# Rounding half of g by GpSimd DMAs, weights' signs by ScalarE, a state updated in place, and another written order

## The chip, the cores and the metric

The kernel runs on one core of one Trainium2 chip. A core has TensorE (PE in the profile; its weight loads are PEld), VectorE (DVE), ScalarE (ACT), GpSimd (POOL) and SyncE (SP), each with a queue that it works through in order, and 16 DMA engines that move data for all of them. The metric is device microseconds of one execution. Before the change the median of three runs was 516.24 us (515.70 to 516.78).

## The reference, cut to what matters

There are two stages. The first is a gated linear recurrence for 4 batches and 8 heads over 768 tokens of 48 numbers; the second a gated two-layer network on 3072 tokens.

```python
for t in range(S):
    state = alpha[:, :, t, :, None] * state + einsum('bhd,bhe->bhde', k[:, :, t], v[:, :, t])
    y[:, :, t] = einsum('bhd,bhde->bhe', q[:, :, t], state)
x = y.transpose(0, 2, 1, 3).reshape(3072, 384)
h = x @ w_in                                   # 384 x 2048
sp = maximum(h, 0) + log1p(exp(-abs(h)))       # softplus
g = h * erf(sp)
out = g @ w_out                                # 2048 x 384
```

q, k, v and alpha are float32; the two weights come as float64.

## The kernel before

**Tiles.** The tokens are cut into 24 chunks of 128 (64 tokens of two batches) and 12 blocks of 256 (two chunks). The 2048 hidden columns of a block are 4 groups of 512 rows by 256 tokens (a tile of 128 x 1024), each of two halves (128 x 512).

**High and low parts.** Every large product runs on TensorE with operands rounded to float32r. A number is split into a rounded part and the rest, and three products are added: high x high, low x high, high x low. `hm` (line 532) is one half's h: 3 x 6 matmuls of 256 columns into a PSUM ring of two. `om` (617) is one half's share of the output: 3 x 4 matmuls of 384 columns.

**One chunk** (`la` to `xe`, lines 296 to 465): loads; two scans over alpha (`sb`, `sa`); scaled k and q (`kk`, `qq`); k transposed (`pn`, then `kn` by ScalarE or `kd` by VectorE); the state scaled by the chunk's whole decay (`td`) and put to use for the outputs (`qt`); products within the chunk (`ps`, masked by `mk`, `sv`); the state's new part (`pu`) added (`ta`). `outputs` (372) opens a PSUM tile with `qt` or `sv` and closes it with the other; between the two stands a `relay`, a memset on GpSimd that waits for the first. The result goes to x by `xh` (the rounded part, by ScalarE) and `xl` (the rest, by VectorE); a second way to the rest, `xp` with `xe` (TensorE subtracts, ScalarE copies), is defined, and the order does not use it. The state has two tiles per batch pair: `td` writes the second from the first, `ta` the first from the second.

**One group** (lines 532 to 631): `hm`, copied by `he` (ScalarE) or `hd` (VectorE); `u`, `n1`, `n2`, `n3`, `g` on ScalarE, 1024 columns each; `ma`, `mb`, `z1`, `z2` on VectorE, `z2` leaving g in the h tile. `u` and `g` need one table set of ScalarE, `n1` to `n3` another; `need` (259) loads a set where the one before was the other. g's high part, `gh`, is written by `ga` (ScalarE) or `gd` (VectorE), the rest by `gl` (VectorE), both into rings of two tiles, and `om` follows. `oe` (ScalarE) or `ob` (VectorE) copies out and `od` stores.

**Weights** (644 to 727). 12 tiles of w_in (`i`, 512 columns) and 16 of w_out (`o`, 384 columns) are loaded as pairs of 32-bit words (`wl`) and made float32 by bits: `wy` scales the upper word, `wc` (ScalarE) or `wv` (VectorE) takes three bits from the lower one, `wa` shifts and joins them, `wb` puts the sign back. `wh` (ScalarE) or `wk` (VectorE) rounds; the low part comes by `wq` (VectorE) or by `wp` (TensorE) with `we` (ScalarE). `wd` and `wf` are defined and not used in the order: `wd` writes the upper 16-bit half of each word, which leaves the sign, `wf` the lower half, with the three bits.

**Order.** `ORDER` (line 31) lists all 1664 steps. Each of the queues of TensorE, VectorE, ScalarE and SyncE issues its instructions in just that order (`Queue`, 203). GpSimd's instructions are not held to it. `dw` steps are matmuls on a constant whose result nobody uses. The rest of the program (`general`) runs only where a check of the values fails; with these inputs it does not.

Of the kernel before, what the change touches and what calls it, by code (L numbers as in the profile page):

```python
# [31 lines left out]
la_0 wli_2 wyi_2 wci_2 wli_3 wyi_3 wci_3 sb_0 rc_0 sa_0 wai_2 wbi_2 whi_2 wli_0 wyi_0 wci_0 wai_3 wbi_3 dw_14  # L32
wpi_2 lk_0 kk_0 wli_4 whi_3 wyi_4 lq_0 ic_0 la_1 wci_4 wei_2 wai_0 wbi_0 pn_0 kn_0 whi_0 wpi_3 wei_3 qq_0 dw_3
ps_0 wai_4 wli_7 wci_7 wli_6 sb_1 mk_0 wyi_7 wbi_4 wai_7 wci_6 wyi_6 wli_8 wpi_0 rc_1 whi_4 dw_7 wpi_4 wbi_7
whi_7 wai_6 sa_1 wbi_6 wyi_8 wci_8 wai_8 lv_0 ic_1 wei_4 wli_5 lq_1 qq_1 wei_0 lk_1 pu_0 kk_1 wli_1 lv_1 wci_5
sv_0 xh_0 wyi_5 xl_0 wbi_8 wpi_7 wai_5 whi_6 ps_1 mk_1 wci_1 wyi_1 wai_1 whi_8 wei_7 wlo_2 wpi_6 wvo_2 sv_1
wyo_2 xh_1 wbi_1 whi_1 wei_6 wpi_8 ta_0 la_2 sb_2 wao_2 wlo_12 wyo_12 dw_1 wpi_1 pn_1 wei_8 wbi_5 whi_5 wpi_5
wli_11 wco_12 kn_1 wbo_2 wei_1 wli_9 who_2 rc_2 ic_2 xl_1 wei_5 sa_2 hm_0_0_0 wao_12 td_2 lq_2 wyi_11 wbo_12
wlo_0 lk_2 wco_0 wqo_2 lv_2 wli_10 who_12 hm_0_0_1 kk_2 pu_1 qq_2 ps_2 wqo_12 wyo_0 wao_0 wci_9 wci_11 wai_11
he_0_0_0 la_3 sb_3 wbi_11 wbo_0 wci_10 wyi_10 he_0_0_1 wai_10 wyi_9 wai_9 lk_3 hm_0_1_0 mk_2 qt_2 u_0_0 rc_3  # L40
hm_0_2_0 sv_2 lq_3 ta_1 wbi_9 sa_3 wlo_1 wbi_10 he_0_1_0 whi_11 whi_9 who_0 td_3 wqi_11 la_4 qq_3 wvo_1 kk_3
wqo_0 he_0_2_0 whi_10 wyo_1 wao_1 sb_4 wqi_9 n1_0_0 xh_2 xl_2 pn_2 kn_2 n2_0_0 wqi_10 ic_3 hm_0_1_1 he_0_1_1
n3_0_0 hm_0_2_1 he_0_2_1 wbo_1 rc_4 who_1 pu_2 ps_3 wlo_3 wyo_3 lq_4 lk_4 wlo_7 mk_3 ta_2 qt_3 ma_0_0 g_0_0 sa_4
wlo_6 mb_0_0 wqo_1 hm_0_3_0 z1_0_0 wco_3 wao_3 lv_3 sv_3 xh_3 xl_3 kk_4 pn_3 he_0_3_0 wyo_7 hm_0_3_1 kn_3 ic_4
z2_0_0 td_4 lk_5 he_0_3_1 la_5 wco_7 wco_6 hm_1_0_0 qq_4 wlo_9 wyo_6 sb_5 u_0_1 wao_7 wbo_3 ga_0_0_0 gl_0_0_0
hm_1_1_0 he_1_0_0 ga_0_0_1 gl_0_0_1 wao_6 u_0_2 n1_0_1 pu_3 ps_4 n1_0_2 rc_5 n2_0_1 qt_4 om_0_0_0 hm_1_0_1 wbo_7
# [97 lines left out]
def gla_moe(ctx: ExitStack, tc: tile.TileContext, q, k, v, alpha, w_in, w_out, out):  # L144
    nc = tc.nc
# [57 lines left out]
    class Queue:  # L203
# [3 lines left out]
        def __getattr__(self, name):  # L207
# [57 lines left out]
    for t in Ts[0] + Ts[1]:  # L265
        nc.gpsimd.memset(t, 0.0)  # L266
# [377 lines left out]
    class Weight:  # L644
# [66 lines left out]
        def wk(self):  # L711
            self.wh(on_dve)
# [234 lines left out]
```

## Time and profile before

| | |
|---|---|
| runs, median (lowest to highest) | 516.24 us (515.70 to 516.78) |
| profiled execution, first to last instruction (span) | 513.9 us |
| runs' median over that span | 2.3 us |
| TensorE busy, matmuls | 504.0 us (98%) |
| VectorE busy | 488.2 us (95%), 655 instructions |
| ScalarE busy | 465.8 us (91%), 637 instructions, 64 of them table loads |
| GpSimd busy | 6.5 us (1%) |
| granted clock of TensorE | 1.000 |

The profiled execution has no other time of its own than its span, so the last rows compare it with the runs. A duration is that of one instruction from its start until its result is written; neighbours on an engine overlap by some 0.07 us, so the distance of two starts is what an instruction takes from its queue. A matmul's end is modelled; its start is a record. "idle before" is an engine's idle time and what ended it. All calls pass through a helper, so most instructions bear its line, 211, and are told apart by their tiles: `acc` is the output's PSUM, `h` that of h, `hs` the h and g tiles, `py` and `both` those of the recurrence.

### The profile page before, as it was taken

Reading aid. Unit: us, or ns where it says so; the run is one execution under the profiler, and the core shown is the slowest. Engines: PE = TensorE matmul, PEld = TensorE weight load, DVE = VectorE, ACT = ScalarE, POOL = GpSimd, SP = SyncE. Lnnn points to the kernel's source line nnn. Section 1 sums busy time; section 2 is a strip of 40 time slices with the busy share of each in tenths; the row PEclk is TensorE's granted clock in tenths of the full one; section 3 lists DMA queues with packets and bytes.
Section 4 is the critical chain, followed back from the end, with each engine's and each line's share of the span. In section 5 each row is a group of like instructions: output and inputs, shape, how many; then the busy total and the mean of one; then the engine's idle time right before and its main releaser. Section 6 shows DMA issues by size and latency. Waiting matters only on the chain.

```text
span 513.9 us, 16869 instructions
## 1 busy us (share of the span) xinstructions
PE 504.0 (98%) x7465; PEld 481.7 (94%) x7465; DVE 488.2 (95%) x655; ACT 465.8 (91%) x637; POOL 6.5 (1%) x41
## 2 busy tenths in 40 slices
PE   6999999999999999999999999999999999999996
PEld 6689999999999999999999999999999999999996
DVE  6999999999999999999999999999998999999894
ACT  6999999999999989999898888899988899898992
POOL 3000000000000000000000000000000000000000
PEclk9999999999999999999999999999999999999999
DMA  8954363321121032122023211301231310000000
GB/s 324 401 200 176 117 188 131 97 81 60 58 74 44 22 99 78 45 73 83 23 78 107 80 41 60 85 15 44 68 111 54 90 58 32 3 1 32 0 32 34
DMA packets 21387, 43.69 MB, mean 85 GB/s; under 512 B 2368, under 2 KB 5440, under 8 KB 21312
## 3 DMA queue, kind: packets, MB, share of 16 engines
q1 hardware_dynamic: 21312, 42.59, 25.4%
q8 instruction: 59, 0.97, 0.8%
q14 instruction: 16, 0.13, 0.1%
HBM read 37.86 MB, written 4.72 MB: 83 GB/s over the span
## 4 chain that ended last, share of the span: by engine, by line
PE 64%; DVE 18%; ACT 12%; issue 4%; DMA 1%; POOL 1%; DVEq 0%; POOLq 0%; ACTq 0%
PE acc L211 29%; PE h__112 L211 13%; PE h__111 L211 12%; PE both L211 4%; PE py L211 4%; DVE t L211 2%; DVE gl__104 L211 1%; ACT L211 1%; DVE gl__103 L211 1%; DVE w__98 L211 1%; DVE w__100 L211 1%; PE warm L211 1%; ACT w__97 L211 1%; DMA s__87<-in_moe_w_out_dram 1%; DVE w__97 L211 1%
## 5 line engine op out<-in xcount | busy, mean ns | idle before, releaser
L211 ACT ACT_TABLE_LOAD x64 | 82.1, 1283 | 1.9 <-PEq L901 0.9
L211 PE MATMUL acc<-wo_hi,gh__102 128*128 128x384 f32 x192 | 44.7, 346 | 0.1
L211 PE MATMUL acc<-wo_hi,gh__101 128*128 128x384 f32 x192 | 43.9, 348 | 0.1
L211 PE MATMUL acc<-wo_lo,gh__102 128*128 128x384 f32 x192 | 43.0, 337 | 0.2 <-DVE wo_lo L211 0.2
L211 PE MATMUL acc<-wo_hi,gl__104 128*128 128x384 f32 x192 | 43.1, 337 | 0.0
L211 PE MATMUL acc<-wo_lo,gh__101 128*128 128x384 f32 x192 | 41.6, 336 | 0.0
L211 PE MATMUL acc<-wo_hi,gl__103 128*128 128x384 f32 x192 | 41.6, 337 | 0.0
L211 PEld LDWEIGHTS acc<-wo_lo,gh__102 128*128 128x128 f32 x192 | 34.2, 188 | 0.5 <-DVE wo_lo L211 0.5
L211 PEld LDWEIGHTS acc<-wo_hi,gl__104 128*128 128x128 f32 x192 | 34.3, 188 | 0.0
L211 PEld LDWEIGHTS acc<-wo_hi,gl__103 128*128 128x128 f32 x192 | 34.0, 188 | 0.2 <-DVE gl__103 L211 0.2
L211 PEld LDWEIGHTS acc<-wo_lo,gh__101 128*128 128x128 f32 x192 | 34.1, 188 | 0.0
L211 PEld LDWEIGHTS acc<-wo_hi,gh__101 128*128 128x128 f32 x192 | 31.6, 188 | 1.9 <-DVE gh__101 L211 0.4
L211 PEld LDWEIGHTS acc<-wo_hi,gh__102 128*128 128x128 f32 x192 | 32.6, 188 | 0.8 <-DVE gh__102 L211 0.2
L211 DVE TENSOR_TENSOR_SCAN B<-raw_a,back 128x520 f32<-128x520 f32 x24 | 29.6, 1233 | 4.0 <-POOL T L266 3.9
L211 DVE TENSOR_TENSOR_SCAN A<-raw_a,start 128x520 f32<-128x520 f32 x24 | 29.6, 1233 | 0.2
L211 ACT ACTIVATE s__88<-s__88 128x1024 f32<-128x1024 f32 x22 | 23.2, 1056 | 1.0 <-DVE t L211 0.9
L211 ACT ACTIVATE s__86<-s__86 128x1024 f32<-128x1024 f32 x20 | 21.2, 1058 | 1.9 <-DVE t L211 1.8
L211 PE MATMUL h__112<-x_hi__107,wi_hi 128*128 128x256 f32 x144 | 21.7, 286 | 0.3 <-ACT wi_lo L211 0.3
L211 PE MATMUL h__111<-x_hi__107,wi_hi 128*128 128x256 f32 x144 | 21.4, 284 | 0.0
L211 PE MATMUL h__111<-x_hi__108,wi_hi 128*128 128x256 f32 x144 | 21.1, 282 | 0.0
L211 PE MATMUL h__112<-x_hi__108,wi_hi 128*128 128x256 f32 x144 | 21.1, 282 | 0.0
L211 PE MATMUL h__112<-x_lo__109,wi_hi 128*128 128x256 f32 x144 | 21.0, 281 | 0.0
(338 smaller groups left out, 1420.5 us busy)
## 6 DMA issues: line engine op xcount, KB each, us to landing
raw_a<-in_alpha_dram SPq DMA_DIRECT2D x24, 260.5 KB, 2.8
raw_k<-in_k_dram SPq DMA_DIRECT2D x24, 256.0 KB, 3.1
raw_q<-in_q_dram SPq DMA_DIRECT2D x24, 256.0 KB, 3.3
raw_v__113<-in_v_dram SPq DMA_DIRECT2D x12, 256.0 KB, 3.3
raw_v__114<-in_v_dram SPq DMA_DIRECT2D x12, 256.0 KB, 3.6
out_dram<-o__106 SPq DMA_DIRECT2D x12, 192.0 KB, 2.0
out_dram<-o__105 SPq DMA_DIRECT2D x12, 192.0 KB, 2.6
s__85<-in_moe_w_out_dram SPq DMA_DIRECT2D x4, 384.0 KB, 3.7
```

What stands on the lines that cost most here:

```text
L211: ins = made(*args, **kw)
```

## The change

48 of the 96 high parts of g are written by `gh`, a DMA that GpSimd issues (from float32 to float32r, 256 KB from SBUF to SBUF); 27 stay with ScalarE (51 before) and 21 with VectorE (45). Their ring has four tiles in place of two. GpSimd gets an ordered queue as well, in which the `gh` and the `relay` memsets stand. Of the 28 weights 20 get sign and low bits by `wd` and `wf` and need no `wb`; the rounding goes mostly to VectorE (`wk` 17, from 1), and the low part of 7 comes by `wp` and `we` (9 before), of 21 by `wq` (19). Four chunks take `xp` and `xe` in place of `xl`. The state has one tile per batch pair: `td` and `ta` update it in place. A group's h tile is taken from its ring by the first `he` (the first `hm` before), so either half can come first. The order is another one, of 1666 steps.

```diff
-    gp = Ring(gpool, gh=([P, 2, TB], F32R, 2), gl=([P, 2, TB], F32R, 2), o0=([P, DM], F32, 1), o1=([P, DM], F32, 1))
+    gp = Ring(gpool, gh=([P, 2, TB], F32R, 4), gl=([P, 2, TB], F32R, 2), o0=([P, DM], F32, 1), o1=([P, DM], F32, 1))
...
-    queues = [Queue(e) for e in (nc.tensor, nc.vector, nc.scalar, nc.sync)]
-    pe, dve, act, sp = queues
+    queues = [Queue(e) for e in (nc.tensor, nc.vector, nc.scalar, nc.sync, nc.gpsimd)]
+    pe, dve, act, sp, pool = queues
...
-            dve.tensor_tensor(out=Tv[self.m][1], in0=Tv[self.m][0], in1=ae.unsqueeze(3).broadcast_to([P, NI, NP, D]), op=ALU.mult)
+            dve.tensor_tensor(out=Tv[self.m], in0=Tv[self.m], in1=ae.unsqueeze(3).broadcast_to([P, NI, NP, D]), op=ALU.mult)
...
-                self.relay = nc.gpsimd.memset(relay, 0.0)
+                self.relay = pool.memset(relay, 0.0)
...
-                dve.tensor_tensor(out=Tv[self.m][0], in0=Tv[self.m][1], in1=U, op=ALU.add)
+                dve.tensor_tensor(out=Tv[self.m], in0=Tv[self.m], in1=U, op=ALU.add)
...
+        def to_hi(self, g, half, copy):
             gg = self.hs[g][:, half * 512 : (half + 1) * 512]
             gh = self.pl.gp.tile([P, 2, TB], F32R, name="gh", tag="gh")
-            act.activation(gh.rearrange("p a t -> p (a t)"), gg, AF.Copy)
+            copy(gh.rearrange("p a t -> p (a t)"), gg)
             self.gg[g, half] = gg, gh
 
+        def gh(self, g, half):
+            self.to_hi(g, half, lambda out, in_: pool.dma_start(out=out, in_=in_))
+
+        def ga(self, g, half):
+            self.to_hi(g, half, on_act)
...
+
+        def wm(self):
+            pool.dma_start(out=self.hi, in_=self.z)
```

`wm` stands in the program and not in the order. Two lines of the new order, the first and the first with `gh`:

```
dw_14 la_0 wli_2 wci_2 sb_0 wyi_2 wli_0 rc_0 sa_0 lk_0 wli_3 ic_0 wfi_0 wai_2 wyi_0 kk_0 wlo_3 wbi_2 wdi_0 la_1 wai_0
rc_5 hm_1_2_0 ta_3 sa_5 he_1_2_0 wao_7 gh_0_0_0 sv_4 lq_7 kk_5 xh_4 wqo_1 gl_0_0_0 la_6 pn_4 hm_1_2_1 td_5 om_0_0_0
```

## Rows read from the trace of the kernel before

**Rows 1.** The page, part 1: busy us, share, instructions of each engine.
```profile
PE 504.0 (98%) x7465; PEld 481.7 (94%) x7465; DVE 488.2 (95%) x655; ACT 465.8 (91%) x637; POOL 6.5 (1%) x41
```
**Rows 2.** Stretches: length; busy us (instructions) by engine; clock, DMA share, GB/s.
```profile
0.00:20.00 20.00, 15.64 (x195) 12.66 (x196) 15.51 (x23) 15.60 (x30) 4.38 (x19) 1.00 0.92 353
20.00:40.00 20.00, 19.35 (x349) 14.91 (x348) 20.00 (x36) 19.97 (x42) 0.10 (x1) 1.00 0.68 242
```
**Rows 3.** Waits of TensorE's weight loads, 28.8 to 120 us: total, times, longest.
```profile
PEld h__112 L211 <- ACT wi_lo L211: 0.9, 1, 0.9
...
PEld h__111 L211 <- ACT hs__94 L211: 0.2, 1, 0.2
```
**Rows 4.** Timeline of TensorE at the first `hm`: start us, length us, instruction.
```profile
28.88 0.99 PE L211 MATMUL h__112<-x_hi__107,wi_hi 128*128 128x256 f32 x6 [0.26 <-ACT wi_lo L211]
```
**Rows 5.** Timeline of TensorE at its end.
```profile
509.33 0.51 PE L211 MATMUL acc<-wo_hi,gl__104 128*128 128x384 f32 x2
```
**Rows 6.** Timeline of TensorE, 108 to 116 us: starts of an `hm` and two `om`.
```profile
108.88 0.87 PE L211 MATMUL h__111<-x_hi__107,wi_hi 128*128 128x256 f32 x6
...
111.00 0.87 PE L211 MATMUL acc<-wo_hi,gh__101 128*128 128x384 f32 x4
...
113.12 0.87 PE L211 MATMUL acc<-wo_hi,gh__102 128*128 128x384 f32 x4
```
**Rows 7.** Groups by line: count, busy us, mean ns of one, idle before.
```profile
L211 PE MATMUL py<-raw_q,T 48*32 48x64 f32 x1408 | 18.9, 224 | 0.0
```
**Rows 8.** Timeline of VectorE, 104 to 117 us.
```profile
104.82 1.22 DVE L211 SCALAR_TENSOR_TENSOR w__99<-t,w__99 128x1024 f32<-128x1024 f32 x1
105.96 0.55 DVE L211 TENSOR_TENSOR wo_lo<-w__97,wo_hi 128x384 fp32r<-128x384 f32 x1
...
111.25 0.42 DVE L211 CAST gh__102<-hs__92 128x512 fp32r<-128x512 f32 x1
...
112.05 1.23 DVE L211 TENSOR_TENSOR_SCAN A<-raw_a,start 128x520 f32<-128x520 f32 x1
113.20 0.67 DVE L211 TENSOR_TENSOR gl__104<-hs__92,gh__102 128x512 fp32r<-128x512 f32 x1
...
114.38 0.68 DVE L211 TENSOR_TENSOR raw_k<-raw_k,B 128x512 f32<-128x512 f32 x1
114.98 0.55 DVE L211 TENSOR_TENSOR T<-T,B 128x384 f32<-128x384 f32 x1
115.45 1.22 DVE L211 TENSOR_TENSOR t<-s__86,w__99 128x1024 f32<-128x1024 f32 x1
```
**Rows 9.** Timeline of ScalarE, 13 to 24 us.
```profile
13.33 1.23 ACT L211 ACTIVATE w__97<-hs__94 128x512 int32<-128x512 uint8 x2
14.45 1.25 ACT L211 ACTIVATE w__98<-hs__95 128x512 int32<-128x512 uint8 x2
```
**Rows 10.** Waits over the whole span: VectorE's first instruction.
```profile
DVE B L211 <- POOL T L266: 3.9, 1, 3.9
```
**Rows 11.** Groups by line: ScalarE's table loads, and one group of `ga`.
```profile
L211 ACT ACT_TABLE_LOAD x64 | 82.1, 1283 | 1.9 <-PEq L901 0.9
...
L211 ACT ACTIVATE gh__102<-hs__93 128x512 fp32r<-128x512 f32 x6 | 3.8, 629 | 2.7 <-DVE hs__93 L211 2.7
```
**Rows 12.** DMA issues: count, KB each, median us from issue to landing.
```profile
raw_v__114<-in_v_dram SPq DMA_DIRECT2D x12, 256.0 KB, 3.6
out_dram<-o__106 SPq DMA_DIRECT2D x12, 192.0 KB, 2.0
out_dram<-o__105 SPq DMA_DIRECT2D x12, 192.0 KB, 2.6
...
hs__95<-in_moe_w_in_dram SPq DMA_DIRECT2D x2, 512.0 KB, 7.0
```
**Rows 13.** Waits over the whole span: the `relay` memsets.
```profile
POOL relay L395 <- PE py L211: 439.8, 22, 32.3
```

More of the change, by code (lines that the diff above doesn't have):

```diff
@@ L37 @@
[L37 to L46, printed above, removed]
@@ new lines @@
+z2_4_2 gl_4_1_0 om_4_1_0 ta_13 ga_4_2_0 mk_14 gl_4_2_0 xl_13 z1_4_3 gl_4_0_1 ic_15 u_5_2 n2_5_0 hd_5_3_0 ga_4_2_1
+om_4_2_0 sa_15 n3_5_0 qq_15 om_4_0_1 n2_5_1 ma_5_0 pn_14 mb_5_0 qt_14 kn_14 n1_5_2 ps_15 n3_5_1 z2_4_3 pu_14 hd_5_3_1
+td_15 sv_14 ma_5_1 lq_16 gl_4_2_1 ga_4_3_1 gl_4_3_1 u_5_3 hm_6_1_1 g_5_0 hm_6_1_0 mb_5_1 he_6_1_1 z1_5_0 mk_15
+he_6_1_0 la_16 gh_4_3_0 u_6_1 od_3_0 om_4_2_1 sb_16 g_5_1 n2_5_2 z2_5_0 n1_5_3 hm_6_0_0 rc_16 z1_5_1 gd_5_0_0 z2_5_1
+hm_6_2_1 om_4_3_1 ic_16 gl_4_3_0 sa_16 om_4_3_0 gh_5_1_1 od_3_1 n3_5_2 n1_6_1 he_6_0_0 n2_5_3 xh_14 oe_4_1 lk_16
@@ new lines @@
+ma_10_0 z1_10_2 he_11_0_1 g_10_0 z2_10_2 f1 om_9_2_1 u_11_0 gh_10_2_0 od_8_1 z2_10_1 mb_10_0 n1_11_0 om_9_0_1
+hm_11_2_0 ga_9_2_0 gl_9_2_0 ma_10_3 hd_11_2_0 hd_11_1_0 n2_11_0 z1_10_0 mb_10_3 om_9_2_0 ga_10_1_1 n3_11_0 ob_9_1
+oe_9_0 ma_11_0 g_10_3 hm_11_1_1 hm_11_2_1 gh_10_2_1 hd_11_1_1 gl_10_2_0 z1_10_3 g_11_0 gl_10_1_1 he_11_2_1 om_10_2_0
+z2_10_3 om_10_1_1 u_11_2 gl_10_2_1 om_10_2_1 z2_10_0 u_11_1 od_9_0 mb_11_0 n1_11_1 hm_11_3_1 hm_11_3_0 ga_10_0_0
+gh_10_3_1 od_9_1 gl_10_0_0 ga_10_0_1 n2_11_1 z1_11_0 gd_10_1_0 n3_11_1 z2_11_0 om_10_0_0 n1_11_2 he_11_3_1 gl_10_3_1
@@ new lines @@
+ma_11_1 mb_11_1 gl_10_0_1 n2_11_2 n3_11_2 om_10_0_1 he_11_3_0 g_11_1 gh_10_3_0 om_10_3_1 ma_11_2 z1_11_1 z2_11_1
+g_11_2 gl_10_1_0 gh_11_0_1 mb_11_2 gl_10_3_0 u_11_3 om_10_1_0 om_10_3_0 z1_11_2 n1_11_3 ob_10_1 n2_11_3 gl_11_0_1
+gh_11_0_0 gl_11_0_0 oe_10_0 z2_11_2 f2 ga_11_1_1 f3 ga_11_1_0 n3_11_3 om_11_0_1 om_11_0_0 od_10_0 gl_11_1_1 gh_11_2_0
+ga_11_2_1 gl_11_1_0 ma_11_3 om_11_1_0 mb_11_3 om_11_1_1 od_10_1 g_11_3 z1_11_3 gl_11_2_0 z2_11_3 om_11_2_0 gh_11_3_1
+gl_11_2_1 gd_11_3_0 om_11_2_1 gl_11_3_0 om_11_3_0 gl_11_3_1 om_11_3_1 oe_11_1 ob_11_0 od_11_1 od_11_0
@@ L262, in need @@
             act.preload_act_table_set(name)
-    Ts = [[at.tile([P, NI * NP * HD], F32, name="T", tag=f"T{m}{n}", bufs=1) for n in range(2)] for m in range(M)]
-    for t in Ts[0] + Ts[1]:
+    Ts = [at.tile([P, NI * NP * HD], F32, name="T", tag=f"T{m}", bufs=1) for m in range(M)]
+    for t in Ts:
         nc.gpsimd.memset(t, 0.0)
-    Tv = [[t.rearrange("p (i a d) -> p i a d", i=NI, a=NP)[:, :, :, :D] for t in pair] for pair in Ts]
+    Tv = [t.rearrange("p (i a d) -> p i a d", i=NI, a=NP)[:, :, :, :D] for t in Ts]
     both = ps_at.tile([P, 2, 512], F32, name="both", tag="b")
     pe.matmul(
-        out=both[:, 1, NP * TC : NP * (TC + D)], lhsT=ident, rhs=Ts[0][0][:, : NP * D],
+        out=both[:, 1, NP * TC : NP * (TC + D)], lhsT=ident, rhs=Ts[0][:, : NP * D],
         start=True, stop=True,
@@ L402, in left @@
                 r0, at0 = (par ^ i) * HD, (i * NP + pair) * HD + d0
-                return Ts[self.m][1][r0 : r0 + D, at0 : at0 + 32], r0
+                return Ts[self.m][r0 : r0 + D, at0 : at0 + 32], r0
             self.outputs(left, lambda i, par, pair: self.Q[(par ^ i) * HD : (par ^ i) * HD + D, pair, i, :])
@@ L533, in hm @@
             x_hi, x_lo = self.x
-            if half == 0:
-                self.hs[g] = self.pl.h.tile([P, GT * TB], F32, name="hs", tag="hs")
             self.ph = self.pl.ph.tile([P, 512], F32, name="ph", tag="h")
@@ L549, in he @@
         def he(self, g, half, copy=on_act):
+            if self.hs[g] is None:
+                self.hs[g] = self.pl.h.tile([P, GT * TB], F32, name="hs", tag="hs")
             sl = slice(half * 512, (half + 1) * 512)
@@ L594, in z2 @@
             )
-        def ga(self, g, half):
+        def to_hi(self, g, half, copy):
             gg = self.hs[g][:, half * 512 : (half + 1) * 512]
             gh = self.pl.gp.tile([P, 2, TB], F32R, name="gh", tag="gh")
-            act.activation(gh.rearrange("p a t -> p (a t)"), gg, AF.Copy)
+            copy(gh.rearrange("p a t -> p (a t)"), gg)
             self.gg[g, half] = gg, gh
+        def gh(self, g, half):
+            self.to_hi(g, half, lambda out, in_: pool.dma_start(out=out, in_=in_))
+        def ga(self, g, half):
+            self.to_hi(g, half, on_act)
         def gd(self, g, half):
-            gg = self.hs[g][:, half * 512 : (half + 1) * 512]
-            gh = self.pl.gp.tile([P, 2, TB], F32R, name="gh", tag="gh")
-            dve.tensor_copy(out=gh.rearrange("p a t -> p (a t)"), in_=gg)
-            self.gg[g, half] = gg, gh
+            self.to_hi(g, half, on_dve)
         def gl(self, g, half):
```

185 lines of the change are left out of this document (86 added, 99 removed).

## The prediction, made before the changed kernel ran

> **What bounds the kernel now.** I read the page's busy shares first, then the stretches, the waits of TensorE, and its timeline at two places. TensorE is busy 98% of the span, VectorE 95%, ScalarE 91% [rows 1]; three engines at the wall say that the share of none of them settles it, so the stretches come next. In the first 20 us TensorE has 15.64 us of work recorded, part of it `dw` matmuls that compute nothing, and from 20 us on it is full, at granted clock 1.00, the higher of its levels [rows 2]. The waits of its weight loads from 28.8 to 120 us come to 2.4 us in five rows, 0.9 us the largest (the first and the last stand in [rows 3]). So behind the first `hm` (which starts at 28.88 us [rows 4]) TensorE hardly stops. The last matmul ends at 509.84 us [rows 5]: 509.84 - 28.88 = 480.96 us for what follows the first `hm`. The kernel is therefore two terms: how late the first `hm` comes, and the 481 us behind it, in which VectorE must keep up closely enough.
>
> I check that by summing TensorE's steps behind that point in the written order. One `hm` (18 matmuls) goes from 108.88 to 111.00, one `om` (12 matmuls) from 111.00 to 113.12 [rows 6]; 96 of each make 407 us. The 22 `qt` are busy 18.9 us, 0.86 each [rows 7]; by the distance of their starts the attention steps take a little less, `qt` 0.84, `sv` 0.89, `ps` 0.57, `pu` 0.57 and `pn` 0.54 us (five such groups, of which one stands). With 20 to 22 of each the whole is 478.7 us, 2.3 us under the 480.96 taken.
>
> **How I sum the other two engines.** An instruction's slot is the distance between two starts, less than its duration, as neighbours overlap. On VectorE: 1.14 us for 1024 columns (104.82 to 105.96), 1.15 for a scan (112.05 to 113.20), 0.60 for 512 (114.38 to 114.98), 0.47 for 384 (114.98 to 115.45), 0.36 for a cast of 512, which the trace records at 0.42 [rows 8]. On ScalarE two conversions of 512 take 1.12 us, 0.56 each (13.33 to 14.45) [rows 9]; I use 0.48 to 0.56 for 512 columns by kind and three quarters of that for 384.
>
> **Term 1: ScalarE's queue ahead of the first `hm`.** Before, the last that it waits for there is `we` of weight i1; after, `xe` of chunk 1. Counting ScalarE's steps ahead of it, before to after: `wc` 10 to 2, `wd` and `wf` 0 to 5 each, `we` 8 to 7, `wh` 9 to 1, `wy` 11 to 10, `xe` 0 to 2, `ic` 2 to 3. That is nine fewer of 512 columns (9 x 0.52 = 4.7) and three more of 384 (3 x 0.42 = 1.3), so 22.3 us become 19.0 us, -3.3. The 16-bit half writes (`wd`, `wf`) have no row. The nearest is `wc`, which also reads one byte in eight, at 0.56 us; I take that, and as the far bound twice it. VectorE's queue to the same place goes from 22.1 to 20.1 us (ten `wb` become two, six casts take the place of `wh`), so ScalarE stays last. TensorE's work behind the point goes from 478.7 to 478.0 (two `xp` more, one `ps` and one `pu` fewer; the three `wp` saved, net two, lie ahead of it, where TensorE waits anyway). By this term alone the end moves by -3.3 - 0.7 = -4.0 us.
>
> **Term 2: VectorE's queue up to the first `om` of block 1.** This is where VectorE is tightest. Before, the second `gl` of that group runs from 113.20 us [rows 8] and its `om` from 113.12 [rows 6], whose last four matmuls want it: hardly any margin. VectorE's slots up to it sum to 108.5 us, and with its start at 3.92 us [rows 10] to 112.4, against 113.87 in the trace. After, up to the first `gl` of the same group: `wb` 28 to 8 (-10.4), `xl` 7 to 3 (-1.9), `gl` 10 to 9 (-0.6); against it 16 more casts `wk` (+5.1), `wq`/`wv` (+1.8), and attention that now runs earlier, `sb` and `rc` +1, `kk` +2, `qq`, `mk`, `ta`, `kd`, `gd` +1, `td` +2 (+5.9). Sum 108.4: the same. But TensorE has less left behind it: `hm` 74 to 72, `om` 87 to 88, one `pn`, `ps`, `qt`, `sv` fewer: -4.24 + 2.10 - 2.84 = -5.0. So this term moves by -5.1, to 502.9 from 508.0; the first term stands at 501.9 from 505.9. The later one decides: -5.1.
>
> **What is off that path.** ScalarE loses 24 `ga` (0.63 us recorded, 0.52 in slots: -12.5) and gets ten more table loads (63 to 73 switches in the written order, 1.29 us each by 1283 ns recorded: +12.9) [rows 11], so the DMAs pay for the tables. VectorE loses 24 `gd`, 10 us in all by the whole balance. Both gains lie mostly after 165 us, where TensorE is behind by its own sums: they buy no time, only margin. The state in place makes `ta` wait for TensorE's `qt`; in 18 of 20 chunks `pu`, for which `ta` waits anyway, stands behind `qt` on TensorE, and in the other two 8 and 16 us of matmuls stand between `qt` and `ta`: nothing, and if that cover went, one `qt` (0.84 us). In the last steps the second `o` goes to VectorE, but both output DMAs queue behind ScalarE's copy: some 0.3 us either way, put at zero.
>
> **The DMAs that round g.** 48 `gh` are issued by GpSimd; the trace has none. Let L be the time from the end of `z2` to data for `gl`: GpSimd's wake, issue, 256 KB through the DMA engines, and the wait's end. Nearest rows: 192 KB out of SBUF land 2.0 and 2.6 us after SP issues them, 256 KB loads 3.6, and at the slow end 512 KB loads 7.0 [rows 12]. As 256 KB move between two places in SBUF I take the SBUF rows plus 64 KB and GpSimd's own issue, L = 3.2 us; bounds 2.0 and 7.0. While L passes, VectorE needs other work: the slots between `z2` and `gl` in the new order, for the 16 `gh` up to 165 us, are 3.9, 10.0, 3.4, 4.0, 8.6, 6.4, 2.9, 3.8, 2.8, 2.7, 3.3, 4.0, 4.6, 5.2, 3.3, 12.6 us. What L lacks there is VectorE standing still with all that is queued behind: 0.4 + 0.4 + 0.5 at L = 3.2, of which the last two fall where term 2 has 0.9 us of margin. I charge 0.6. After 165 us VectorE leads and the same shortfall is hidden.
>
> [...]
>
> In the same queue stand the 22 `relay` memsets, each of which waits for TensorE's `qt` (439.8 us of waiting in all [rows 13]); a `gh` behind one waits until TensorE is there. Counting TensorE's work from each such `qt` to the `om` that needs the `gh`, the shortest is 5.4 us, against L plus one `gl`, 3.8: hidden. A `gh` also waits until the `om` four tiles back has freed its buffer; the tightest of these (g of block 11, group 0) has 4.2 us of matmuls between, against the same 3.8.
>
> **Sum.** -5.1 + 0.6 = -4.5 us on the profiled execution: its span of 513.9 becomes 509.4. The runs' median, 516.24, lies 2.3 us over that span; with the same around it the forecast is 511.7 us.
>
> **Rivals.** (a) Eaten up: L is about 4.0. The shortfalls are then 0.1, 0.6, 1.2, 0.2, 1.2, 1.3 and 0.7 = 5.3 us, less 0.9 of margin: 515.5 us. For it: loads run beside the first eight `gh`, and a loaded queue shows 3.6. Half writes at twice `wc`'s slot (ten of them, +5.4 on term 1, its margin 1.0) end at the same 515.5, and so does a first `hm` that waits for weights, not for ScalarE: DMA is 0.92 busy in the first 20 us [rows 2], so term 1 might not move. Against the last: 5.4 MB are issued up to the last weight it needs, 6.6 before.
> (b) The other side: L is 5.0. Then the shortfalls up to 165 us are 13.5 us (two halves of one `z2` wait together), less 0.9: 516.24 - 5.1 + 12.6 = 523.7. It decides from L = 4.2 on: at 4.5 the same count gives about 520. For it: GpSimd's issue is in no row, and one queue serves all 48. Against: the transfers that leave SBUF land within a median of 2.6 us.
>
> [...]
>
> (c) It doesn't do what it says: the lead of term 2 holds but other waits of a new order take it back in the 480 us behind; the old order has 2.3 us of them, twice as many would make 514.0.
>
> **Chances.** Forecast, with (c) as its weak form: 0.62, own range 509.5 to 514.5. (a) 0.17. (b) 0.21. A measurement of this kernel can tell 0.2%, 1.03 us, from no change: faster is below 515.2, slower above 517.3. Half of (a) falls on either side of 515.2, near enough: faster 0.67, same 0.11, slower 0.22. The range goes from 509.5 (no shortfall, fewer waits) to 519.5 (L just under 4.5), leaving out 0.05 below and 0.14 above; the far bound of L, 7.0, lies out there.
>
> **What would show it.** First `hm` near 25.6 us (term 1); 478 us of TensorE behind it; `gl` of block 1's first group ending near 114 us with one `om` and no `pn`, `ps`, `qt`, `sv` left over as counted; GpSimd's issues landing within 3 us, and VectorE's waits for DMA under 2 us before 165 us. I am wrong if VectorE's waits name `gh` for 5 us or more in that stretch, if `wd` and `wf` take a microsecond, or if the first `hm` still starts after 28 us.

## The result: slower, by 1.0 to 2.0%

The changed kernel takes 523.62 us in the median of four runs (521.01 to 527.62) against 516.02 beside it (515.70 to 516.78): a ratio of 1.0146, 95% interval 1.0097 to 1.0195. A second set of five gave 522.53 us, ratio 1.0128 (1.0112 to 1.0144). The forecast was 511.7, and the time lies outside the range too. The profiled execution (span 519.3, time 521.01) is the fastest of the nine runs.

The page of the changed kernel, part 1, and its first stretches and the one from 105 to 185 us (the columns of [rows 1] and [rows 2]):

```profile
PE 503.5 (97%) x7467; PEld 482.8 (93%) x7467; DVE 473.3 (91%) x633; ACT 464.6 (89%) x621; POOL 31.4 (6%) x87
```

```profile
0.00:20.00 20.00, 16.07 (x197) 13.05 (x198) 14.93 (x25) 15.15 (x30) 3.45 (x17) 1.00 0.88 329
20.00:40.00 20.00, 19.11 (x448) 16.31 (x446) 17.84 (x31) 17.89 (x38) 0.23 (x1) 1.00 0.81 289
40.00:60.00 20.00, 18.83 (x355) 18.13 (x359) 18.61 (x33) 19.32 (x33) 0.20 (x2) 1.00 0.47 164
...
105.00:185.00 80.00, 77.46 (x1239) 74.01 (x1231) 75.36 (x96) 73.31 (x98) 5.65 (x14) 1.00 0.36 101
```

VectorE lost 15 us of work against [rows 1], and ScalarE 1. Nobody got faster by it: from 20 to 40 us, where both were full before [rows 2], they now stand still for 2 us each, and TensorE for 0.9 (0.65 before). In the two later stretches the kernel before has these rows, with TensorE at 20.00 and 79.75:

```profile
40.00:60.00 20.00, 20.00 (x503) 19.10 (x481) 20.00 (x32) 19.91 (x36) 0.20 (x2) 1.00 0.55 187
...
105.00:185.00 80.00, 79.75 (x1086) 76.91 (x1087) 78.60 (x99) 78.53 (x100) 0.29 (x3) 1.00 0.20 61
```

The first `hm` and the last matmul of the changed kernel (timeline, as [rows 4] and [rows 5]):

```profile
26.37 0.68 PE L205 MATMUL both<-raw_q,raw_k 48*64 48x64 f32 x27 [0.16 <-issue]
26.98 0.98 PE L205 MATMUL h__114<-x_hi__109,wi_hi 128*128 128x256 f32 x6
...
513.26 0.51 PE L205 MATMUL acc<-wo_hi,gl__106 128*128 128x384 f32 x2
```

The first `hm` comes 1.9 us earlier, not 3.3, and follows TensorE's own `ps_2` without a wait for ScalarE. From there to the end of the last matmul (513.77) it is 486.8 us, not 480.3: 8.8 us over the 478.0 us of work, where the old order had 2.3. Of the 8.8 us the trace shows 6.1 as idle time of TensorE, of the 2.3 it shows 1.1; the rest is in longer distances between its starts. From the last matmul to the end of the span it is 5.5 us, 4.1 before; the second output's issue comes 1.0 us after that matmul (514.75), 0.6 before:

```profile
514.33 0.34 SPq L205 DMA_DIRECT2D out_dram<-o__108  x1
514.75 0.42 SPq L205 DMA_DIRECT2D out_dram<-o__107  x1
```

The longest of what TensorE waited for from 24 us on (total us, times, longest; "issue" is a wait for nothing that the profile shows):

```profile
PE py L205 <- issue: 1.5, 3, 1.0
PE acc L205 <- DMA gh__103<-hs__95: 1.1, 1, 1.1
PE acc L205 <- DMA gh__103<-hs__90: 1.0, 1, 1.0
PE h__114 L205 <- ACT hs__90 L205: 0.8, 1, 0.8
PE acc L205 <- DMA gh__103<-hs__96: 0.6, 1, 0.6
PE py L205 <- ACT x_lo__112 L205: 0.5, 1, 0.5
```

DMA issues, as [rows 12]: two kinds of loads, one of the two outputs of a block, and two groups of the 48 transfers. One by one the transfers land 2.3 to 6.0 us after their issue. The loads land later than before, `raw_a` at 3.8 us where it is 3.0 and 3.4 without the transfers (e2 and e5 below); the outputs are as late without them (2.8 us in e2):

```profile
raw_a<-in_alpha_dram SPq DMA_DIRECT2D x24, 260.5 KB, 3.8
...
raw_v__115<-in_v_dram SPq DMA_DIRECT2D x12, 256.0 KB, 4.8
...
out_dram<-o__107 SPq DMA_DIRECT2D x12, 192.0 KB, 2.8
...
gh__101<-hs__96 POOLq DMA_DIRECT2D x3, 256.0 KB, 2.5
...
gh__103<-hs__95 POOLq DMA_DIRECT2D x1, 256.0 KB, 5.6
```

**One number for every place.** To compare orders I take, at a TensorE step, its start plus the slots of all TensorE steps still to come (`hm` 2.12, `om` 2.10, `sv` 0.89, `qt` 0.84, `pu` and `ps` 0.57, `pn` 0.54, `xp` 0.25 us): where its matmuls would end with no further wait. It rises where TensorE loses time, by waiting or by a lower clock. In us, at 70, 105 and 185 us, with the kernels of the experiments below:

| kernel | first `hm` | at 70 | at 105 | at 185 | last matmul | span |
|---|---|---|---|---|---|---|
| before | 28.9 | 507.5 | 507.9 | 509.0 | 509.8 | 513.9 |
| changed | 27.0 | 507.0 | 508.2 | 511.7 | 513.8 | 519.3 |
| e4, changed again | 29.4 | 510.1 | 510.7 | 514.5 | 517.1 | 522.7 |
| e5, 44 transfers gone | 27.6 | 508.5 | 509.2 | 509.6 | 511.8 | 517.2 |
| e8, old to 107 us, then new | 29.7 | 508.3 | 508.6 | 514.2 | 516.8 | 522.4 |
| e11, old order with 25 transfers | 28.9 | 507.6 | 507.9 | 508.8 | 508.6 | 513.1 |
| e14, mended | 26.3 | 505.7 | 506.7 | 508.9 | 511.1 | 515.6 |

Changed against before, by stage: -0.5 up to 70 us, +0.8 to 105, +2.4 to 185, +1.2 to the last matmul, +1.5 behind it: together the spans' 5.4.

### The profile page after: what moved, and what is told of

Its sections match the earlier page's. It is cut to its first block, busy times and chain, and to the rows that moved or that the text cites. A ratio compares the mean times of both kernels' runs of the same rounds, so it can differ in the third digit from the quotient of the medians.

```text
span 519.3 us, 16979 instructions
## 1 busy us (share of the span) xinstructions
PE 503.5 (97%) x7467; PEld 482.8 (93%) x7467; DVE 473.3 (91%) x633; ACT 464.6 (89%) x621; POOL 31.4 (6%) x87
## 4 chain that ended last, share of the span: by engine, by line
PE 49%; DVE 15%; ACT 5%; DMA 4%; issue 3%; DVEq 0%; POOLq 0%; ACTq 0%; POOL 0%
PE acc L205 23%; PE h__114 L205 10%; PE h__113 L205 10%; PE py L205 4%; PE both L205 3%; DVE t L205 2%; DVE gl__105 L205 1%; DVE w__99 L205 1%; DMA gh__103<-hs__95 1%; DVE gl__106 L205 1%; ACT L205 1%; DMA raw_a<-in_alpha_dram 1%; ACT w__99 L205 1%; DMA gh__103<-hs__90 1%; DVE s__87 L205 1%
## 5 line engine op out<-in xcount | busy, mean ns | idle before, releaser
L205 ACT ACT_TABLE_LOAD x74 | 94.9, 1283 | 2.1 <-PEq L901 0.9
L205 PE MATMUL acc<-wo_hi,gl__106 128*128 128x384 f32 x192 | 43.8, 340 | 0.3
L205 PE MATMUL acc<-wo_hi,gl__105 128*128 128x384 f32 x192 | 41.3, 337 | 0.0
L205 DVE TENSOR_TENSOR_SCAN B<-raw_a,back 128x520 f32<-128x520 f32 x24 | 29.7, 1238 | 7.2 <-POOL T L260 3.9
L205 PEld LDWEIGHTS acc<-wo_hi,gl__106 128*128 128x128 f32 x192 | 33.9, 188 | 1.7 <-DVE gl__106 L205 1.7
L205 PEld LDWEIGHTS acc<-wo_hi,gl__105 128*128 128x128 f32 x192 | 34.0, 188 | 0.1
L205 DVE TENSOR_TENSOR_SCAN A<-raw_a,start 128x520 f32<-128x520 f32 x24 | 29.7, 1238 | 0.1
L205 PE MATMUL acc<-wo_hi,gh__103 128*128 128x384 f32 x96 | 22.3, 341 | 2.6 <-DMA gh__103<-hs__95 1.1
L205 ACT ACTIVATE s__88<-s__88 128x1024 f32<-128x1024 f32 x20 | 21.2, 1058 | 2.3 <-DVE t L205 2.2
L205 ACT ACTIVATE s__86<-s__86 128x1024 f32<-128x1024 f32 x20 | 21.1, 1055 | 2.3 <-DVE t L205 2.2
L205 PE MATMUL h__114<-x_hi__110,wi_hi 128*128 128x256 f32 x144 | 21.8, 287 | 0.8 <-ACT hs__90 L205 0.8
L205 PE MATMUL h__114<-x_hi__109,wi_hi 128*128 128x256 f32 x144 | 21.8, 287 | 0.2 <-ACT hs__95 L205 0.2
L205 PE MATMUL acc<-wo_lo,gh__103 128*128 128x384 f32 x96 | 21.9, 336 | 0.0
L205 PE MATMUL h__113<-x_hi__110,wi_hi 128*128 128x256 f32 x144 | 21.7, 287 | 0.0
L205 PE MATMUL h__113<-x_hi__109,wi_hi 128*128 128x256 f32 x144 | 21.7, 286 | 0.0
L205 PE MATMUL acc<-wo_hi,gh__104 128*128 128x384 f32 x96 | 21.3, 339 | 0.0
L205 ACT ACTIVATE s__87<-s__87 128x1024 f32<-128x1024 f32 x20 | 21.1, 1057 | 0.2
L205 PE MATMUL acc<-wo_hi,gh__101 128*128 128x384 f32 x96 | 21.2, 339 | 0.0
L205 PE MATMUL acc<-wo_lo,gh__104 128*128 128x384 f32 x96 | 21.1, 337 | 0.0
L205 PE MATMUL h__113<-x_hi__109,wi_lo 128*128 128x256 f32 x144 | 21.0, 281 | 0.0
L205 PE MATMUL h__113<-x_hi__110,wi_lo 128*128 128x256 f32 x144 | 20.9, 281 | 0.0
L205 PE MATMUL h__114<-x_hi__110,wi_lo 128*128 128x256 f32 x144 | 20.9, 281 | 0.0
```

Source lines behind the costliest of these rows:

```text
L205: ins = made(*args, **kw)
```

## The experiments

Each was timed beside the kernel before (515.9 to 516.3 us in all sets). My first theory, A, was the transfers: VectorE and TensorE wait for rounded data. Against it stood B, the new order's other waits; C, the changed code; and D, for the spread of the runs, TensorE's clock.

**e1 to e4: code, transfers, the short ones, and the kernel again.** e1 is the changed code with the old `ORDER`. e2 and e3 change words of the new one:

```diff
-  ... gh_0_0_0 ... gh_11_3_1 ...      (48)
+  ... gd_0_0_0 ... gd_11_3_1 ...      (e2: all 48; e3: 12 of them)
```

> The changed kernel's code (four gh buffers, state updated in place, relay on the ordered GpSimd queue) with the order of the kernel before, so no gh DMA and the old forms of the weights. Theory A (the 48 gh transfers cost the time: VectorE and TensorE wait for data that lands 3 to 6 us after z2): 516.0, as before. Theory B (the other waits of the new order, DMAs or not): 516.0 too. Theory C (in-place state or the ordered GpSimd queue costs): half or more of the 7.6 us, 519 or above, with VectorE waits for T or raw_q that the kernel before does not have.

515.65 us, ratio 0.9985 (0.9976 to 0.9994). The state in place, four tiles and GpSimd's ordered queue cost nothing; theory C is out.

> The changed kernel with all 48 gh transfers made VectorE copies (425 ns each, +20.4 us of VectorE work, 473 to 494 us busy) at the same places of the order. Theory A: the 4.4 us that TensorE loses behind gh data (om_0_1_1, om_1_3_1, om_2_0_0, the last blocks) and most of the lower clock go, time 517 to 519. Theory B (the order's other waits: first blocks, PSUM hand-overs, tail): no better than the changed kernel, 523 or above, the copies' own delay on top.

524.10 us, ratio 1.0163 (1.0143 to 1.0183). Taken alone this says that the transfers are innocent. But VectorE went from 473.3 to 488.5 us, and TensorE, which lost 3.5 us between 105 and 185 behind transfers, lost 3.3 there, its longest waits now for `gl`, `kn` and `T` (0.3 to 0.6 us each). One cost stood in for the other, so e5 was needed.

> The changed kernel with only the 12 gh transfers made VectorE copies whose gl starts within 5 us of z2 or waited for them (of blocks 0, 1, 2, 6, 8, 9, 11); the other 36 stay transfers. Theory A in its narrow form (latency without cover, not traffic): as good as without any transfer or better, 517 to 519.5, TensorE's stalls at 86, 152 and 166 us gone. If the traffic of the transfers itself costs (slower loads, landing times): 521 or above. Theory B: 523 or above.

522.45 us, ratio 1.0132 (1.0110 to 1.0154), no better than the changed kernel. The waits at 152 and 166 us were gone, and from 105 to 185 us its profile loses 2.1 us instead of 3.5. But it stood at 509.1 already at 70 us (507.0 in the changed kernel's first profile), part of it by a lower clock (below), so this run does not price the 12 transfers.

> The changed kernel again, for a second profile and its clock. Theory D (each us over 520.5 is TensorE's granted clock falling behind a stall): the runs with a mean clock of 1.000 take 520 to 521, each 0.001 of clock below adds 0.5 us, and a profile with a clock under 0.997 shows half speed right behind one of the stalls at 45, 152, 166, 460 or 497 us. Otherwise: times spread at one clock.

522.53 us (521.97 to 524.54). Theory D holds in part. The profiled run was 3.4 us longer than the first profile, and 3.1 of that stood already at 70 us (table). That was not the clock, which stayed at 1.00 up to 517 us: TensorE stopped for 2.2, 1.0 and 1.3 us up to 48 us (0.2, 0 and 1.1 at the same places in the first profile), with nothing shown that it waits for; e13 and the last section come back to these stops. Time did not follow the clock alone in the other runs either: 522.21 at 1.000, 521.97 at 0.998. A stretch where the clock did fall is seen in e3's profile, around its first `hm` at 28.4 us:

```profile
25.00:27.00 2.00, 1.36 (x41) 0.94 (x40) 2.00 (x6) 2.00 (x5) 0.00 (x0) 1.00 0.82 261
27.00:29.00 2.00, 1.24 (x32) 1.17 (x32) 2.00 (x4) 2.00 (x5) 0.00 (x0) 1.00 0.96 309
29.00:33.00 4.00, 4.00 (x23) 4.00 (x23) 3.21 (x7) 2.75 (x6) 0.00 (x0) 0.57 0.99 322
```

TensorE had stood still for a third of 4 us; then its granted clock is 0.57 on average for 4 us (0.50 from 30 to 32 us), and 1.7 us of the first `hm`'s lead are gone.

**e5: neither transfers nor copies.**

```diff
-            self.to_hi(g, half, lambda out, in_: pool.dma_start(out=out, in_=in_))
+            if self.tok == 0 and g < 2:
+                self.to_hi(g, half, lambda out, in_: pool.dma_start(out=out, in_=in_))
+            else:
+                self.to_hi(g, half, lambda out, in_: on_dve(out[:, :8], in_[:, :8]))
```

> The changed kernel with 44 of its 48 gh transfers (all but the first four) made VectorE copies of 8 columns instead of 512, so that neither a transfer nor 20 us of VectorE work stands in their place; the high parts of these tiles are then not computed. Theory A (transfers, or, in the run without them, the copies' VectorE work): both gone, TensorE's waits at 150 to 170 us gone, 517 to 518.5. Theory B (the new order's own waits: first blocks, PSUM hand-overs between the engines, tail): 520 or above, with stalls of 0.3 to 1.5 us where the two runs with other high parts have theirs.

519.69 us, ratio 1.0065 (1.0051 to 1.0080): between the two. From 105 to 185 us TensorE now loses 0.4 us; its row there, and that of the changed kernel above, 79.64 against 77.46 busy:

```profile
105.00:185.00 80.00, 79.64 (x1304) 77.30 (x1303) 79.37 (x111) 76.34 (x104) 0.39 (x4) 1.00 0.23 68
```

So the transfers are worth some 3 us (3.5 and 3.8 lost in this stretch in the two profiles of the changed kernel, 0.4 here), nearly all between 105 and 185 us: behind 185 us e5 loses as much as the changed kernel (table). The other 3.6 us over the kernel before belong to the new order without them.

**e6 to e8: which part of the order.** The order is cut at one step: up to it one order, then what is left in the other (weights that had begun keep their form).

```diff
- ORDER = new
+ ORDER = new up to hm_0_0_0, then old      (e6)
+ ORDER = new up to om_0_3_1, then old      (e7)
+ ORDER = old up to om_0_3_1, then new      (e8)
```

> The changed kernel's order up to and including the first hm, then the order of the kernel before for what is left (no gh transfer in it; the weights that had begun keep their new forms). The step of the prediction on its own: first hm at 25.6 us and TensorE bound behind it gives 516.0 - 4.0 = 512. Theory B: the lead stands at the first hm (27 to 28 us) and TensorE keeps it in the old order: 513.5 to 515. Theory E (the early stage is bound by the load of the weights, so a lead at the first hm is lost before 55 us in any order): 515.5 to 516.5.

520.00 us, ratio 1.0072 (1.0059 to 1.0085): all three numbers missed. The new order reaches the first `hm` with fewer weights done, and in the old order the postponed conversions stand on ScalarE in front of the `he` that frees the `h` tile for `hm_0_1_0`. TensorE's wait there, and ScalarE's timeline (`hs__95` is the `he`):

```profile
PE h__114 L205 <- ACT hs__95 L205: 3.8, 1, 3.8
```

```profile
35.96 0.52 ACT L205 ACTIVATE wo_hi<-w__100 128x384 fp32r<-128x384 f32 x1
36.38 0.54 ACT L205 ACTIVATE w__98<-s__88 128x384 f32<-128x384 f32 x1
36.82 1.38 ACT L205 ACTIVATE w__99<-hs__92 128x512 int16<-128x512 uint8 x2
38.07 0.63 ACT L205 ACTIVATE w__97<-hs__93 128x512 int32<-128x512 uint8 x1
38.60 0.58 ACT L205 ACTIVATE hs__95<-h__114 128x512 f32<-128x512 f32 x1
```

Its granted clock was down twice besides (0.57 on average from 29 to 33 and from 39.5 to 43.5 us), behind a stop of 1.4 us at 28.7 and behind this one, which is another 3.4 us. In this run the lead at the first `hm` is borrowed from what comes next. The seam makes this case extreme; it does not price the lead in the new order itself.

> The changed kernel's order up to the last om of block 0 (about 107 us, 7 of the 48 transfers), then the order of the kernel before. Projected from the two traces: the changed kernel stands 0.3 us behind the kernel before at 105 to 120 us, so 516 to 517 if the loss is behind this point (Theory B late, or A). If the first 107 us hold the loss: 519 or above.

524.46 us, ratio 1.0170 (1.0154 to 1.0187), but 8 us of it are the seam (waits of 1.6 and 3.9 us for `gh` tiles at 119 and 130 us, and a granted clock of 0.54 from 129 to 136.5), so the time decides nothing; its first 105 us, at 510.1, are one more sample of the new order.

> The order of the kernel before up to the last om of block 0 (about 107 us), then the changed kernel's order with 41 of the 48 transfers. The counterpart: what the changed order costs behind 107 us, 3 us of TensorE's waits at 150 to 170, 1 at 460, 1 at 497, 1.4 of tail: 521 to 523 by theory B or A; 517 or below if the loss is in the first 107 us.

524.21 us, ratio 1.0160 (1.0147 to 1.0174). Up to 105 us the run is the kernel before (508.6); behind it the new order loses 8.2 us, the old one 1.9. About 2 of that may be the seam (109 to 123 us); 2.9 are waits of the changed kernel at the same steps, 1.05 and 1.08 us for transfers at 155 and 168 and 0.78 at 463. The tail is 5.6.

**e9 and e10: two mends, each alone.**

```diff
- gl_1_3_1 z1_2_1 om_1_3_0 he_3_2_0 om_1_3_1 sb_10 lq_10 z2_2_1 hm_3_3_1
+ z1_2_1 gl_1_3_1 om_1_3_0 he_3_2_0 sb_10 lq_10 z2_2_1 hm_3_3_1 om_1_3_1
  (e9; gl_2_0_0 behind ma_2_2 and om_2_0_0 behind hm_4_0_0 likewise)
- oe_11_1 ob_11_0 od_11_1 od_11_0
+ oe_11_0 od_11_0 ob_11_1 od_11_1
  (e10; and xl for xp and xe in chunks 0, 1, 2, 5)
```

> The changed kernel with all 48 transfers; for two of the three late ones, gl moves one VectorE step back (gl_1_3_1 behind z1_2_1, gl_2_0_0 behind ma_2_2, 1.2 us each) and om one TensorE step back (om_1_3_1 behind hm_3_3_1, om_2_0_0 behind hm_4_0_0, 2.1 us each). Theory A as latency without cover: TensorE's waits of 1.1 to 1.6 us at 152 and of 1.1 us at 166 us go and nothing takes their place, 522.5 - 2.3 = 520.2. If the transfers cost by traffic (or VectorE merely gets later elsewhere): no gain, 522 or above.

522.12 us, ratio 1.0120 (1.0106 to 1.0135). Half of it came true. The wait at 152 us is 0.2; the other has only changed hands: the `hm` put ahead of the late transfer waits as long for its `h` tile.

```profile
152.05 0.98 PE L205 MATMUL h__114<-x_hi__110,wi_hi 128*128 128x256 f32 x6 [0.20 <-ACT hs__95 L205]
...
165.30 0.98 PE L205 MATMUL h__114<-x_hi__109,wi_hi 128*128 128x256 f32 x6 [1.10 <-ACT hs__96 L205]
```

> The changed kernel with two edits, read apart in the trace: the end of the kernel before (half 0's copy and output ahead of half 1's), and for chunks 0, 1, 2 and 5 the lower half of x by one VectorE subtraction instead of TensorE's xp and ScalarE's xe. The first takes the 1.4 us that the stretch from the last matmul to the end grew by (5.5 back to 4.1); the second 4 x 0.25 = 1.0 us of TensorE, unless VectorE, later by 4 x 0.55 us, delays the first blocks by as much. Together 520.1 to 521.5 against 522.5; 522 or above if the end is set by something else.

521.26 us, ratio 1.0105 (1.0088 to 1.0122). The tail is 4.5 us, 1.1 less. The 1.0 us of TensorE work saved is not seen: at 70 us it stands at 507.4, the changed kernel at 507.0.

**e11: transfers with cover, in the old order.** e1 with 25 of its copies made transfers right behind `z2` or the release of their tile, for example

```diff
- z2_5_0 ... gd_5_0_0 gl_5_0_0
+ z2_5_0 gh_5_0_0 ... gl_5_0_0
```

> The order of the kernel before with 25 of its copies (9 of VectorE, 16 of ScalarE) made gh transfers, each put right behind z2 or the release of its buffer, where the profile of that order leaves at least 6 us to gl. Theory A as latency without cover: these transfers cost nothing, 515.0 to 515.9 (against 515.65 without them), TensorE without a wait for gh. If transfers cost by their traffic on the DMA engines: 517 or above, with raw_a and raw_v landing later.

515.46 us, ratio 0.9988 (0.9978 to 0.9998). Between 30 and 512 us the waits name TensorE not once, although these transfers land no faster:

```profile
gh__104<-hs__94 POOLq DMA_DIRECT2D x3, 256.0 KB, 5.4
...
gh__102<-hs__95 POOLq DMA_DIRECT2D x1, 256.0 KB, 5.5
```

So the traffic of these 25 costs nothing, and with cover (6 us or more from `z2` to `gl` for each) their latency does not either. All but one are issued behind 150 us, so this says nothing of transfers beside the loads of the weights. With e1 (515.65) this is the fastest version: both lie 0.12 to 0.15% under the kernel before, at the edge of what can be told.

**e12 and e13: TensorE's waits for nothing that is shown.** In ten profiles whose order is the new one up to 55 us, nine have such a wait of 0.5 to 1.6 us behind TensorE's matmul number 728, five one of 0.6 to 2.2 behind 346, two one of 0.7 to 1.0 behind 474 (the expectations count from zero).

```diff
- dw_14 la_0 ...
+ dw_14 ds_64 la_0 ...     (e12: 64 small matmuls more)
- dw_3 wai_3 dw_7 wyo_3 ...
+ dw_3 wai_3 wyo_3 ...     (e13)
```

> The changed kernel with 64 small matmuls (some 0.9 us of an idle TensorE) more right behind the first warm-up. Theory F: TensorE's waits for nothing that the profile shows come where its instructions run out, 128 matmuls apart (counted over all matmuls, they were ahead of number 346 in ps_2, 474 in pn_2 and 728 in sv_3, the same in each run of this order), while loads keep the DMA engines over nine tenths busy. The waits then come at the same numbers, now other steps: none of 0.8 us or more in ps_2 and sv_3, one of 0.5 to 2 us near number 602 (in sv_2) instead. If they wait for data of these steps: still in ps_2 and sv_3, now numbers 410 and 792. The time is no test: 520 to 525 either way.

529.20 us: a miss twice over. The trace counts each of these float32 matmuls twice (the 14 of the first warm-up show as 28), so the shift was 128, one full spacing, and the wait, at 856, tells nothing. And they took 6 us, which came through whole: first `hm` at 34.1, time 6.7 us up on e4's.

> The changed kernel without one of its warm-ups (dw_7: 14 matmuls as the trace counts them, all ahead of 16 us). The 64 matmuls of the last run count as 128 in the trace, so they moved the count by exactly one spacing and told nothing of where the waits come from. Theory F (TensorE's instructions run out every 128): the waits stay at the numbers 346, 474 and 728 of the stream, which are now the 19th matmul of ps_2, the 11th of sv_2 and the 17th of sv_3. If TensorE waits for data of these steps: at ps_2's 5th, pn_2's first and sv_3's third, as before, now numbers 332, 460 and 714. Time 521 to 524 either way.

521.14 us, ratio 1.0108 (1.0088 to 1.0128). Theory F holds as to where TensorE stops. The timeline of `sv_3`, first in the changed kernel (numbers 726 to 728), then in e13 (712 to 728):

```profile
43.22 0.30 PE L205 MATMUL py<-sT,raw_v__116 64*32 64x64 f32 x3
44.57 0.83 PE L205 MATMUL py<-sT,raw_v__116 64*32 64x64 f32 x61 [1.05 <-issue]
```

```profile
43.65 0.35 PE L205 MATMUL py<-sT,raw_v__116 64*32 64x64 f32 x17
45.63 0.71 PE L205 MATMUL py<-sT,raw_v__116 64*32 64x64 f32 x47 [1.63 <-issue]
```

The wait kept its number and left its place in the step; in `ps_2` likewise, 0.99 us behind its 19th matmul, number 346. The one at 474 did not show in this run. A wait of 1.1 us with the same label ahead of `sv_1` belongs to its step: it is the step's first matmul in every profile that has it, whatever its number.

**e14: the waits mended together.** e9's move of `om_1_3_1`, e10's end, `hm_11_1_0` behind `om_9_2_1`, and

```diff
- gh_0_1_1 ... gh_2_0_0 ... gh_11_3_1
+ gd_0_1_1 ... gd_2_0_0 ... gd_11_3_1
```

> The changed kernel with the waits found so far mended one by one: gl_1_3_1 and om_1_3_1 one step back (1.2 us), the transfers gh_0_1_1, gh_2_0_0 and gh_11_3_1 made VectorE copies (0.6 + 1.1 + 0.5 us less 3 x 0.4 of VectorE), hm_11_1_0 behind om_9_2_1 (0.8 us), the end of the kernel before (1.1 us). If the account is complete, the sum of these, 4 to 5 us, comes off 522.6: 518 to 519, still 2 to 3 above the kernel before by the early lead that is lost and the lower clock. If the waits only move on: 521 or above.

519.98 us (517.23 to 524.28), ratio 1.0079 (1.0045 to 1.0113): 2.6 of the 4 to 5 us. In the profiled run (517.35) it loses 2.2 from 105 to 185 us instead of 3.5, the tail is 4.5; `hm_11_1_1` now waits 0.7 where `hm_11_1_0` did. Part of the waits moved on.

## Why the prediction was wrong

**The step that failed** is the one under Sum and rival (c): that behind the first `hm` TensorE goes on with the old order's 2.3 us of waits. It has 8.8. The view that gave the 2.3 was a trace of the old order, and nothing in it says what a new order waits for. I summed each queue's work and let the longest decide; in the new order no queue is full, and most of the waits shown are for a transfer or for another engine. Rival (c) named this, at twice the 2.3, which was too little by half. In the profiled execution the forecast span, 509.4, was missed by 9.9 us: 6.5 by these waits, 1.4 by a first `hm` later than term 1 had it, 1.5 by the tail, and 0.5 because the sum went by term 2 and not by term 1.

**Term 1** had the sign right and half the size. Over the ten profiles the first `hm` comes at 27.7 us (26.3 to 29.4), over the four that begin in the old order at 29.3 (28.9 to 29.7): -1.6, not -3.3. The half writes are slower than their model. On 512 columns they take 776 to 852 ns where `wc` takes 667 and 677 (the nearest pair stands below), and 0.64 us from start to start where 0.56 was taken: some 0.8 us on the ten. Ahead of the same point ScalarE also stood idle 0.8 us more than before, mostly for one `wp` of TensorE:

```profile
L205 ACT ACTIVATE w__98<-hs__94 128x512 int16<-128x512 uint8 x1 | 0.8, 776 | 0.0
L205 ACT ACTIVATE w__99<-hs__92 128x512 int32<-128x512 uint8 x1 | 0.7, 677 | 0.2 <-DMA hs__92<-in_moe_w_in_dram 0.2
```

```profile
15.22 0.60 ACT L205 ACTIVATE wi_lo<-h__114 128x512 fp32r<-128x512 f32 x1 [0.85 <-PE h__114 L205]
```

Nothing of the lead is left at 70 us: 507.85 us on average (505.7 to 510.1) against 507.95. In the changed kernel's two profiles and e9's, 1.6 to 2.3 us of that went at the waits behind numbers 474 and 728 and at `qt_3`, which waits 0.5 us for `x_lo`. The stops of the kind that e13 tested come to 1.9 us up to 55 us on average over the ten profiles and to less than 0.1 over the four that begin in the old order. They go far to rank the ten: e2 with none and e14 with 0.5 us stand lowest at 70 us, at 506.1 and 505.7, the changed kernel's second profile with 4.5 us highest, at 510.1. Why the same stop takes 0.2 us in one execution and 2.2 in another is not settled.

**Term 2**, -5.1, decided the sum and has no part in the result. It set VectorE's slots against the work that TensorE has left, and left out, but for the 0.6 us of L, that VectorE itself might wait. The first `gl` of block 1's first group ended at 118.8 us, not near 114. VectorE's work up to it was as counted (busy 108.7 us, and 109.0 before up to the second `gl` there), but it stood idle 10.1 us, 4.9 before, which takes the 5 us back whole. 3.9 us at the start are common to both; its other waits up to there, the largest first, and the `gl`:

```profile
DVE B L205 <- DMA raw_a<-in_alpha_dram: 2.4, 3, 1.4
DVE t L205 <- ACT w__97 L205: 1.4, 1, 1.4
DVE wi_lo L205 <- ACT wi_hi L205: 0.8, 1, 0.8
DVE gl__105 L205 <- DMA gh__103<-hs__96: 0.7, 1, 0.7
```

```profile
118.14 0.66 DVE L205 TENSOR_TENSOR gl__105<-hs__92,gh__101 128x512 fp32r<-128x512 f32 x1
```

Nor did TensorE wait for that `gl`: its `om` begins at 118.3 us with no idle time before it, so VectorE's queue was not what ended last there. From 105 to 185 us VectorE stands still for another 4.6 of 80 us (1.4 before).

**L** was well sized for most and wrong as one number. From `z2` to `gl` the quick ones take 2.8 to 3.0 us, 3.2 was taken; the one at 146 us takes 6.2, with two loads of q issued just ahead of it. VectorE's waits for `gh` up to 166 us are 5.0 us in all, the bound I had set for being wrong (3.2 in the second profile); the two largest:

```profile
DVE gl__106 L205 <- DMA gh__103<-hs__95: 2.0, 1, 2.0
DVE gl__105 L205 <- DMA gh__103<-hs__90: 1.6, 1, 1.6
```

By e5 this is some 3 us, where 0.6 was charged (the terms named there, 1.3 less 0.9 of margin, give 0.4). That rival (b) hit the total, 523.7, is luck: its mechanism has less than half of it.

VectorE's casts did not hold up GpSimd's issues in the changed kernel's trace: 47 of the 48 take 0.53 or 0.54 us. During four of these 47 VectorE was running a cast for `gd` (0.42 us), at 109, 117, 337 and 508 us, and their data landed 2.3 to 2.4 us after the issue, among the fastest.

**Off the path**, the state in place is free (e1, 515.65 us), and the ten more table loads cost what was counted, 94.9 against 82.1 us. The tail, put at zero, cost 1.5 us: the output whose copy is done first is now issued last (e10's end takes 1.1 back). `xp` for `xl` added 1.0 us of TensorE work over the whole, and undoing it gave nothing.

## What to carry to other kernels

A gain in one queue's work is a gain only if the end follows that queue; where three engines are each some 90% busy, price a new order by its hand-overs, and do not take the waits of the old order for those of the new one. Place the step that needs a transfer behind the slowest landing on its queue (here 6.0 us), not behind the typical one (2.3 to 3): in e11, with 6 us or more of cover, the transfers were free (515.46 us, 515.65 without them). To test a suspected cost, take it out without putting another in its place: e2 acquitted the transfers, e5 convicted them.

## What the runs showed that I had not expected

TensorE stops at fixed numbers of its instruction stream, and the traces show a load of instructions ahead of the end of each. The waits moved with the count of matmuls, not with the step (e13). Counted with each matmul's weight load and with the semaphore instructions between them, the stops behind numbers 346, 474 and 728 come after 704, 961 and 1473 instructions: 256 apart, and three times that, to within one. These three are not alone: all the traces together, of the old order and the new, have 38 stops over 0.15 us that are marked "issue" and lie at 192 or 193 beyond a multiple of 256. One of the places is in `sv_19` at 366 us, far behind the loads of the weights; it takes 0.15 to 1.3 us there. The other 17 marked so lie elsewhere, each ahead of the first matmul of its step.

The queue that the changed kernel's page names `instruction` (q8) shows 0.97 MB in 59 packets, 16.4 KB each, one for 254.5 of TensorE's 15017 instructions. Each of the 38 stops ends 1.2 to 1.6 us after such a packet has landed. In the changed kernel one runs from 42.08 to 43.04 us, and TensorE stands from 43.52 to 44.57; in e13 it runs from 43.23 to 44.16, and TensorE stands from 44.00 to 45.63. That TensorE waits there for its own instructions is my reading of this; no run changed their loads. The stops lie where small matmuls follow each other closely: 64 take 0.85 us, as the trace counts, and so 256 instructions 1.7 us, while from the start of a packet to the end of a stop it is 2.2 to 3.2 us. In the old order, with its `hm` between them, none is over 0.35 us. Whether the loads beside them make these waits longer was not tried.
